# Turning the third group's alpha, q and k and the fourth group's alpha on four 64x64 tiles of TensorE

## The chip, the core and the metric

The kernel runs on one core of a Trainium2 chip. The core has five engines that run side by side and wait for each other through semaphores: TensorE (PE in the profile, with its weight loads as PEld), VectorE (DVE), ScalarE (ACT), GpSimd (POOL) and SyncE (SP, which here only issues DMAs). The metric is the time of one execution on the device, in microseconds; the kernel before took 270.44 us (median of 3 runs, 270.08 to 271.02).

## The reference

Two blocks follow each other. The first is a gated linear recurrence over 768 steps, for 4 batches and 8 heads of 48 numbers each. The second is a projection with a scalar decay, a gate and an output projection.

```python
for t in range(S):                       # attention block: B, H, S, D = 4, 8, 768, 48
    state = alpha[:, :, t, :, None] * state + np.einsum('bhd,bhe->bhde', k[:, :, t], v[:, :, t])
    y[:, :, t] = np.einsum('bhd,bhde->bhe', q[:, :, t], state)
x = y.transpose(0, 2, 1, 3).reshape(B, S, H * D)
proj = x @ w_in                          # 384 -> 2 * 512
val, gate = proj[..., :512], proj[..., 512:]
for t in range(S):
    h = np.exp(A_log)[0] * h + val[:, t, :]
    ys[:, t, :] = h
out = (gate * (1 / (1 + np.exp(-gate))) * ys) @ w_out
```

## The kernel before, in words

The work is cut into 12 groups of 256 steps: 4 batches with 3 groups each, counted m = 0 to 11. The recurrence of a group is done as matrix products: with running products of alpha, P (forward) and V (backward), q is scaled by P and k by V, then TensorE forms scores, masks them, multiplies by v, and carries a state from one 64-step part to the next. The second block of group n (`project`, four parts cc = 0 to 3, and `output`) runs on TensorE while the recurrence of group n + 1 is prepared.

The inputs arrive with steps along the free dimension: a raw tile has partition 4c + h (c one of 32 runs of 8 steps, h one of 4 heads) and, along the free dimension, the head group i (0 or 1), the step j in the run (0 to 7) and the 48 numbers d. The products need the numbers along partitions and the steps along the free dimension, so every alpha, q and k is *turned*. From the fifth group on (and for the k and q of the fourth) VectorE does it with 32x32 transposes (`turn`). For the first groups TensorE does it: it multiplies by an identity matrix (`ident`), the result lands in PSUM, and ScalarE copies it out in the order of the steps (`copy_turned`, line 714).

`turned` (line 697) turns half of a tensor, four of the eight steps j, into one PSUM bank. It has two ways. By matmul (line 707) each step j takes two products, one for each head group i: all 128 partitions of 64 columns of the raw tile are the weights, and the 128 columns of the identity move through, so a product fills 64 output partitions by 128 columns. By transpose (lines 702 and 703) a step takes two transposes. `turn_over` (line 764) calls it for the first four steps, copies the bank out, and then does the other four in a second bank. Its callers are `alphas` and `straighten`: alpha of group 1 (by transpose), k of group 0 (by transpose), and, what matters here, alpha (line 707), k and q (line 707) of group 2 and alpha of group 3 (by transpose, lines 702 and 703). The first alpha of all has a routine of its own, `first_alphas` (line 723), that works on 64x64 tiles.

Everything in this part of the kernel stands in an order written out by hand: each engine works through its own list, and no scheduler moves anything. Around the change, in the pass n = 0 of the main loop, TensorE's list is: `project(0, 0)`, alpha of group 2, `project(0, 1)`, scores of group 1, k of group 2, q of group 2, half of `project(0, 2)`, values across and states of group 1 (lines 834 and 866), the other half of `project(0, 2)`, alpha of group 3, the rest of group 1's values with the carried states (`third`: lines 847, 834, 847), and then, in the pass n = 1, scores of group 2 (line 798, 32 instructions into the banks s0 and s1 and 32 into two banks mm) and `project(0, 3)`. VectorE's list in the same stretch is: masks of group 1 (line 808), P of group 2 (line 635), V of group 2 (line 654), part of a weight's conversion (lines 549 and 551), the scan of `project(0, 2)` (line 995), four sums of states (line 894), and k and q of group 2 times V and P, in halves (lines 619 and 610); the scores of group 2 read these.

There are four PSUM banks mm0 to mm3 that are handed out in a written order (`taken`). k of group 2 takes banks 1 and 0, q of group 2 takes 2 and 3, `project(0, 2)` takes 1 and 0 and alpha of group 3 takes 2 and 3. SyncE issues the loads in their written order too; the raw tile of a tensor may be filled again once it has been turned.

Of the kernel before, what the change touches and what calls it, by code (L numbers as in the profile page):

```python
# [13 lines left out]
AF = mybir.ActivationFunctionType  # L14
# [332 lines left out]
def fast(  # L347
# [22 lines left out]
    nc = tc.nc  # L370
    B, H, S, D = q.shape
# [24 lines left out]
    NJ = GC // 32  # L396
    ROW = NJ * D
# [18 lines left out]
    def steps_of(name, m):  # L416
        return raws[name][:, ds(m % 2 * (2 * ROW + 16), 2 * ROW + 16)]
# [50 lines left out]
    ident = const.tile([C, C], FP32, name="ident")  # L468
# [127 lines left out]
    def by_runs(t):  # L596
        return t.rearrange("p h (c j) -> p h c j", j=NJ)
# [89 lines left out]
    def bank(tag=None):  # L687
        if tag:
            return ps_at.tile([C, 512], FP32, tag=tag, name=tag)
        return ps_mm.tile([C, 512], FP32, tag=f"mm{next(taken)}", name="mm")  # L690

    def bank_pair(tag=None):
        return [bank(tag and f"{tag}{i}") for i in range(2)]
# [3 lines left out]
    def turned(m, name, js, t, by_transpose=None):  # L697
        raw = steps_of(name, m)
        tp = t[:, 0:len(js) * C].rearrange("p (j x) -> p j x", j=len(js))
        if (m, name) in turned_by_transpose if by_transpose is None else by_transpose:  # L700
            for n, j in enumerate(js):
                nc.tensor.transpose(tp[:, n], raw[:, ds(ROW + j * D - 64, C)], ident)  # L702
                nc.tensor.transpose(tp[0:64, n], raw[:, ds(j * D, 64)], ident)  # L703
            return tp.rearrange("p j (c h) -> p h c j", h=4)
        for n, j in enumerate(js):
            for i in range(2):
                nc.tensor.matmul(tp[ds(64 * i, 64), n], raw[:, ds(i * ROW + j * D, 64)], ident,  # L707
                                 start=True, stop=True, skip_group_check=True)
        return tp.rearrange("p j (c h) -> p h c j", h=4)

    halves = [range(0, NJ // 2), range(NJ // 2, NJ)]

    def copy_turned(to, js, tp):
        nc.scalar.activation(by_runs(to)[:, :, :, js.start:js.stop], tp, AF.Copy)
# [47 lines left out]
        return to  # L762

    def turn_over(m, name, to):
        for js in halves:
            copy_turned(to, js, turned(m, name, js, bank()))

    def alphas(m):
        turn_over(m, "a", by_place(als[m % 2])[:, :, 1:GP])

    def straighten(m, name):
        to = plain(name)
        turn_over(m, name, to)
        return to
# [171 lines left out]
    for h in range(H):  # L946
        i, e, s = h // 4, h % 4 // 2, h % 2 ^ h // 4
# [183 lines left out]
    part = turned(1, "k", halves[0], bank())  # L1131
# [7 lines left out]
    part = turned(1, "k", halves[1], bank())  # L1139
# [9 lines left out]
    part = turned(1, "q", halves[0], bank())  # L1149
# [13 lines left out]
    part = turned(1, "q", halves[1], bank(), False)  # L1163
# [27 lines left out]
    for n in range(N):  # L1191
        m = n + 1
# [223 lines left out]
```

## Time and profile before

| what | value |
|---|---|
| median of 3 runs | 270.44 us (270.08 to 271.02) |
| the profiled execution | 269.92 us |
| span of the profile, first to last instruction | 268.2 us |
| TensorE busy | 263.3 us, 98% of the span |
| VectorE busy | 233.8 us, 87% |
| ScalarE busy | 111.6 us, 42% |
| GpSimd busy | 165.9 us, 62% |
| granted TensorE clock | 1.000 |

The profile is one execution. Its page gives the busy time of each engine, the chain of work that ended last (followed back from the last instruction, at each step to what released it), the costliest groups of instructions by source line, and the DMA issues. The trace behind it answers further questions: the chain in order of time, a timeline of one engine, or the instructions of one line. A row of a timeline reads: start in us, duration in us, engine, line, operation, output <- inputs, count, and in brackets the idle time before it and what ended that. A row that stands for several instructions (x32) runs from the first start to the last end. TensorE executes one fp32 product of the program as two rows of the trace; a transpose is one row. Matmuls are pipelined, so a row of the chain starts where the row before it ends, while the timeline shows the same group a little earlier, from its first start.

### The profile page before, as it was taken

What the parts mean: (1) busy time and instruction counts of PE and PEld (TensorE: products, weight loads), DVE (VectorE), ACT (ScalarE), POOL (GpSimd) and SP (SyncE); (2) the same over time, 40 slices, a digit from 0 to 9 for tenths busy, and PEclk for the clock granted to TensorE, in tenths of its full rate; (3) what the DMA queues carried; (4) which work ended last, traced back from release to release, by engine and by line L of the source; (5) the groups of instructions that cost most, each with busy time, mean ns of one, the idle gap of its engine ahead of it and who ended that gap; (6) DMA issues with size and microseconds to landing.
All of it is one profiled execution on the core that took longest, in us unless ns stands there. A gap on an engine that the chain in (4) does not pass through costs nothing.

```text
span 268.2 us, 9966 instructions
## 1 busy us (share of the span) xinstructions
PE 263.3 (98%) x4168; PEld 230.4 (86%) x4168; DVE 233.8 (87%) x316; ACT 111.6 (42%) x270; POOL 165.9 (62%) x185
## 2 busy tenths in 40 slices
PE   8999999999999999999999999999999999999995
PEld 6898889876688988988988988988988989988874
DVE  7979998996999999799999998999999998883440
ACT  4667766372342542532533533524524515214011
POOL 8222313084169997689985995996876986646000
PEclk9999999999999999999999999999999999999999
DMA  5947984998784569496487488569598501201101
GB/s 177 315 147 242 286 192 154 238 201 194 218 204 112 127 172 218 117 230 155 108 227 167 105 215 182 124 169 212 127 214 170 143 2 31 77 0 39 69 7 59
DMA packets 52304, 41.19 MB, mean 154 GB/s; under 512 B 27392, under 2 KB 50944, under 8 KB 52256
## 3 DMA queue, kind: packets, MB, share of 16 engines
q1 hardware_dynamic: 49328, 37.34, 56.2%
q0 software_dynamic: 1536, 2.20, 3.1%
q10 hardware_dynamic: 1392, 0.99, 1.3%
q8 instruction: 34, 0.56, 0.9%
q14 instruction: 14, 0.11, 0.1%
HBM read 32.54 MB, written 4.72 MB: 139 GB/s over the span
## 4 chain that ended last, share of the span: by engine, by line
PE 91%; DVE 2%; DMA 2%; issue 1%; ACT 1%; POOL 1%; SPq 0%; DVEq 0%; POOLq 0%
PE mm L988 47%; PE mm L1064 16%; PE y L834 4%; PE y L847 4%; PE mm L1022 4%; PE s L798 4%; PE mm L798 3%; PE s L866 3%; DMA raw_q<-in_q_dram 2%; PE mm L1377 2%; PE mm L707 1%; PE mm L702 1%; PE mm L703 1%; DVE P L635 1%; POOL w_in L556 1%
## 5 line engine op out<-in xcount | busy, mean ns | idle before, releaser
L988 PE MATMUL mm<-xT,w_in 128*128 128x256 f32 x576 | 129.5, 382 | 0.1
L988 PEld LDWEIGHTS mm<-xT,w_in 128*128 128x128 f32 x576 | 107.9, 190 | 15.9 <-issue 0.3
L1006 ACT ACTIVATE sg<-mm 128x256 f32<-128x256 f32 x48 | 18.4, 383 | 88.4 <-PE mm L988 85.3
L1008 POOL TENSOR_TENSOR f_last<-sg,hh 128x256 f32<-128x256 f32 x36 | 31.2, 874 | 24.2 <-ACT sg L1006 19.6
L886 POOL TENSOR_TENSOR sum<-sum,dS 128x192 f32<-128x192 f32 x30 | 37.5, 1251 | 3.0 <-ACT dS L874 1.4
L635 DVE TENSOR_TENSOR_SCAN P<-al,lower 128x1028 f32<-128x1028 f32 x12 | 30.3, 2521 | 0.3
L995 DVE TENSOR_TENSOR_SCAN hh<-a_dec,hh,mm 128x256 f32<-128x256 f32 x32 | 23.3, 728 | 7.8 <-PE mm L988 7.5
L654 DVE TENSOR_TENSOR_SCAN V<-al,ends 128x1028 f32<-128x1028 f32 x12 | 28.7, 2391 | 0.4
L963 POOL DMA_DIRECT2D xT<-yst x44 | 22.6, 519 | 4.9 <-ACT yst L960 3.7
L556 POOL TENSOR_TENSOR w_in<-w_in,wr 128x768 int32<-128x768 int32 x4 | 7.3, 1825 | 25.4 <-DVE wr L551 16.1
L1064 PE MATMUL mm<-wide,wr 128*128 128x192 f32 x108 | 20.8, 327 | 0.0
L818 POOL TENSOR_TENSOR AK<-AK,mask 128x512 f32<-128x512 f32 x9 | 15.6, 1729 | 7.7 <-ACT AK L814 7.6
L600 DVE STREAM_TRANSPOSE k<-raw_k 128x1024 f32<-128x1024 f32 x9 | 18.5, 2053 | 0.1
L600 DVE STREAM_TRANSPOSE q<-raw_q 128x1024 f32<-128x1024 f32 x9 | 18.3, 2035 | 0.0
L1064 PEld LDWEIGHTS mm<-wide,wr 128*128 128x128 f32 x108 | 18.0, 190 | 0.0
L874 ACT ACTIVATE dS<-s 128x384 f32<-128x384 f32 (+1 forms) x18 | 7.4, 461 | 22.3 <-PE s L866 22.3
L600 DVE STREAM_TRANSPOSE al<-raw_a 128x1024 f32<-128x1024 f32 x8 | 16.4, 2048 | 0.0
L619 DVE TENSOR_TENSOR Zk<-k,V 128x1024 f32<-128x1024 f32 (+1 forms) x14 | 16.1, 1148 | 0.1
L610 DVE TENSOR_TENSOR Zq<-q,P 128x1024 f32<-128x1024 f32 (+1 forms) x14 | 15.7, 1119 | 0.0
L1064 PE MATMUL mm<-w_out,f_last 128*128 128x192 f32 x72 | 15.6, 339 | 0.0
L847 PEld LDWEIGHTS y<-Zq,sum 48*64 48x64 f32 x656 | 11.6, 134 | 3.5 <-issue 3.2
L834 PEld LDWEIGHTS y<-AK,v 64*64 64x64 f32 x352 | 12.1, 134 | 2.9 <-issue 2.9
(188 smaller groups left out, 504.5 us busy)
## 6 DMA issues: line engine op xcount, KB each, us to landing
v<-in_v_dram SPq DMA_DIRECT2D x22, 192.0 KB, 3.8
out_dram<-o_sb SPq DMA_DIRECT2D x22, 192.0 KB, 2.5
raw_k<-in_k_dram SPq DMA_DIRECT2D x18, 184.0 KB, 4.7
raw_q<-in_q_dram SPq DMA_DIRECT2D x18, 184.0 KB, 4.5
raw_k<-in_k_dram SPq DMA_DIRECT2D x18, 176.0 KB, 5.0
raw_q<-in_q_dram SPq DMA_DIRECT2D x18, 176.0 KB, 4.8
wbits<-in_moe_w_in_dram SPq DMA_DIRECT2D x8, 384.0 KB, 4.9
raw_a<-in_alpha_dram SPq DMA_DIRECT2D x16, 184.0 KB, 3.6
```

Of the source, the lines that this page charges most:

```text
L600: nc.vector.transpose(out=by_runs(to).rearrange("p h c j -> p h j c"), in_=raws[name][:, 0:4 * ROW].rearrange("p (h j d) -> p h j d", h=4, ...
L635: nc.vector.tensor_tensor_scan(out=P, data0=al[:, 0:4 * GP], data1=lower.rearrange("p h t -> p (h t)"), initial=0.0, op0=ALU.mult, op1=ALU ...
L654: nc.vector.tensor_tensor_scan(out=V[:, ::-1], data0=al[:, 1:4 * GP + 1][:, ::-1], data1=ends.rearrange("p h t -> p (h t)")[:, ::-1], init ...
L798: nc.tensor.matmul(scs[m][c][i][ds(L * h, L), ds(p * (L + D), L + D)], Zk[rows, c, p, ds(h * L, L)], Zq[rows, u, p], start=True, stop=True ...
L834: nc.tensor.matmul(ys[m][i][ds(64 * s, 64), e, ds(c * C + h * L, L)], v_sb[rows, c, 4 * i + p, :], As[i][rows, c, p, :], start=across and ...
L847: nc.tensor.matmul(ys[m][i][ds(64 * s, 64), e, ds(u * L, L)], Ss[j][rows, p, :], Zqs[m % 2][rows, u, p, D:], start=False, stop=True, skip_ ...
L886: nc.gpsimd.tensor_add(Ss[j][:, :, 0:D], Ss[j - 1][:, :, 0:D], part)
L963: engines[n % len(engines)].dma_start(out=xT[to, a], in_=st[rows, i, e])
L988: nc.tensor.matmul((pv, pg)[vg], w_ins[cc][:, kk, vg, :], xT[:, kk, :], start=(kk == 0), stop=(kk == NK - 1))
L995: nc.vector.tensor_tensor_scan(out=hh, data0=a_dec[:, cc:cc + 1].to_broadcast([C, GC]), data1=pv, initial=prev_h[cc][:, GC - 1:GC] if n % ...
L1008: f = lambda: engine.tensor_mul(fs[n][cc], sg, hh)
L1064: nc.tensor.matmul(o, a[:, k], b[k] if type(b) is list else b[:, k], start=start and k == 0, stop=k == KC - 1, skip_group_check=True)
```

## The change

`turn_over` keeps the old way for groups 0 and 1. For groups 2 and 3 it takes two banks at once, one for each half of the 128 partitions (r = 0: the first 128 steps of the group, r = 1: the other 128). For each step j it makes four products, one for each pair of head group i and row half r: 64 partitions of 64 raw columns are the weights, and the 64x64 block of the identity on the same partitions moves through. A product fills 64 output partitions by 64 columns of the bank of its row half. When all 32 products of the tensor are listed, ScalarE copies the two banks out, each as 128 consecutive steps. Alpha of group 3 is no longer turned by transposes. The number of copies and the order in which banks are handed out are the same, and no other list changes.

```diff
     def turn_over(m, name, to):
-        for js in halves:
-            copy_turned(to, js, turned(m, name, js, bank()))
+        if m < 2:
+            for js in halves:
+                copy_turned(to, js, turned(m, name, js, bank()))
+            return
+        raw = steps_of(name, m)
+        parts = [t.rearrange("p (j x) -> p j x", x=64) for t in bank_pair()]
+        for j in range(NJ):
+            for i, r in ((0, 0), (1, 1), (1, 0), (0, 1)):
+                rows = ds(64 * r, 64)
+                nc.tensor.matmul(parts[r][ds(64 * i, 64), j], raw[rows, ds(i * ROW + j * D, 64)],
+                                 ident[rows, rows], start=True, stop=True, skip_group_check=True)
+        for r, part in enumerate(parts):
+            nc.scalar.activation(by_runs(to)[:, :, ds(16 * r, 16)], part.rearrange("p j (c h) -> p h c j", h=4), AF.Copy)
```

## The prediction

> **What bounds the kernel now.** I read the page first, for the shares and for the engine that the chain of waits follows.
>
> ```profile
> span 268.2 us, 9966 instructions
> PE 263.3 (98%) x4168; PEld 230.4 (86%) x4168; DVE 233.8 (87%) x316; ACT 111.6 (42%) x270; POOL 165.9 (62%) x185
> PE 91%; DVE 2%; DMA 2%; issue 1%; ACT 1%; POOL 1%; SPq 0%; DVEq 0%; POOLq 0%
> ```
>
> TensorE is busy for 98% of the span and makes up 91% of the chain, so time taken from it ought to come off the end. VectorE, at 87%, is close behind. Averages don't say which of the two is ahead in the stretch that changes, so I then read the chain in order of time, from 25 us on.
>
> ```profile
> 25.37 1.83 POOL w_in L556
> 27.25 2.86 PE mm L988 x12
> 31.80 3.64 PE mm L707 x64
> 35.44 1.49 PE mm L988 x6
> 36.94 0.62 PE y L834 x32
> ...
> 39.77 0.11 PE mm L702
> ...
> 41.41 0.11 PE mm L703
> 41.52 0.39 PE y L847 x16
> 41.91 0.47 PE y L834 x32
> 42.38 0.70 PE y L847 x48
> 43.08 0.77 PE s L798 x32
> 43.85 0.77 PE mm L798 x32
> 44.61 1.49 PE mm L988 x6
> ```
>
> From 27.25 us on every piece is TensorE's and each begins where the last one ends. The turning of k and q (L707, x64) is a piece of 3.64 us; alpha of group 3 (L702 and L703) lasts from 39.77 to 41.52, 1.75 us. Alpha of group 2 is no piece of the chain: before 27.25 stands GpSimd's sum for a weight (L556).
>
> The third view is the stretch from the end of this turning to the end of what can be delayed by it, and asks whether TensorE ever stands after 44.6 us.
>
> ```profile
> 44.60:264.00 219.40, 219.40 (x3232) 192.12 (x3231) 193.94 (x244) 82.63 (x207) 151.12 (x164) 1.00 0.60 141
> ```
>
> The first two numbers are the length of the stretch and TensorE's busy time in it: both 219.40. Whatever TensorE has gained when it starts on `project(0, 3)` at 44.6 us, the end gains too, as long as the other engines follow. So the question is only how much earlier it gets there. The fourth view, VectorE's timeline, answers that.
>
> ```profile
> 32.52 2.58 DVE L635 TENSOR_TENSOR_SCAN P<-al,lower 128x1028 f32<-128x1028 f32 x1
> ...
> 35.56 2.30 DVE L654 TENSOR_TENSOR_SCAN V<-al,ends 128x1028 f32<-128x1028 f32 x1
> ...
> 39.31 1.61 DVE L894 TENSOR_TENSOR sum<-s,sum 128x192 f32<-128x192 f32 x4
> 40.83 0.68 DVE L619 TENSOR_TENSOR Zk<-k,V 128x512 f32<-128x512 f32 x1
> 41.43 0.68 DVE L610 TENSOR_TENSOR Zq<-q,P 128x512 f32<-128x512 f32 x1
> 42.03 0.68 DVE L619 TENSOR_TENSOR Zk<-k,V 128x512 f32<-128x512 f32 x1
> 42.64 0.68 DVE L610 TENSOR_TENSOR Zq<-q,P 128x512 f32<-128x512 f32 x1
> 43.90 0.42 DVE L808 TENSOR_TENSOR A<-s,mask 128x256 f32<-128x256 f32 x1 [0.58 <-PE s L798]
> ```
>
> Up to 43.32 us (42.64 + 0.68) no row carries a bracket: VectorE goes from one instruction to the next without waiting for anybody, and nothing it reads in this stretch comes late. Its next row waits 0.58 us for the scores. TensorE and VectorE are therefore nearly level at 43 us, and TensorE's lead over what VectorE supplies is the measure of what it can gain:
>
> ```profile
> 42.90 0.95 PE L798 MATMUL s<-Zq,Zk 48*64 48x112 f32 x32
> 43.67 0.95 PE L798 MATMUL mm<-Zq,Zk 48*64 48x112 f32 x32
> ```
>
> The second half of the scores of group 2 starts at 43.67 and reads the Zq that is ready at 43.32. That is 0.35 us of room, no more.
>
> **The change part by part.** *One tensor on 64x64 tiles.* 32 products, two rows each: 64 rows in place of 32 (alpha, k and q of group 2), and in place of 16 for alpha of group 3, whose transposes are one row each. TensorE's count grows by 3 x 32 + 48 = 144 rows, to 4312. The nearest rows are the values of L834, which also rotate through all four tiles with 64 columns: 32 in 0.47 us (41.91), 14.7 ns a row, and 0.62 us (36.94) where they follow 128-row work, so 0.15 us for the step into this mode. The other end is the routine that does the same job for the first alpha, at the very start:
>
> ```profile
> 5.13 0.68 PE L723 MATMUL y<-ident,raw_a 64*64 64x64 f32 x26
> L723 PEld LDWEIGHTS s<-ident,raw_a x32: 175/223/228, 3.9 to 5.0; 64*64 64x64 f32 x32
> L723 PE MATMUL y<-ident,raw_a x32: 218/218/311, 4.8 to 5.6; 64*64 64x64 f32 x32
> ```
>
> There 26 rows last 0.68 us; less the 0.218 us of the last one, 25 intervals are 18.5 ns each. All 64 rows of that routine, from 3.9 to 5.81 us, take 30 ns each, the earlier ones with weight loads at 223 ns. I take 14.7 ns, because the new order also changes both the row half and the column half, as L834 does; 30 ns is the upper end.
>
> *k and q:* 128 x 14.7 ns = 1.88 us for 3.64, so 1.76 us less. No step into the mode is added, since L798 before them already runs on parts of the array. *Alpha of group 3:* 64 x 14.7 + 150 = 1.09 us for 1.75, so 0.66 us less. *Alpha of group 2:* gains nothing, as what follows it waits for GpSimd until 25.37 + 1.83 = 27.20, and ScalarE is not free for its copies earlier either:
>
> ```profile
> 26.97 0.36 ACT L1006 ACTIVATE sg<-mm 128x256 f32<-128x256 f32 x1
> 27.23 1.36 ACT L714 ACTIVATE al<-mm 128x512 f32<-128x512 f32 x2
> ...
> 32.64 0.33 ACT L810 ACTIVATE dS<-mm 128x192 f32<-128x192 f32 x1
> 32.87 0.60 ACT L714 ACTIVATE k<-mm 128x512 f32<-128x512 f32 x1
> ...
> 35.49 0.60 ACT L714 ACTIVATE q<-mm 128x512 f32<-128x512 f32 x1 [0.28 <-PE mm L707]
> ```
>
> *Both banks at once.* q needs bank 3 with its second product. Bank 3 is freed by the copy dS, at 32.97; k's tiles would be done at 31.80 + 0.94 = 32.74, so q waits about 0.25 us with the handover (between 0 and 0.3). `project(0, 2)` then starts near 34.0 on banks 1 and 0, and the first copy of k, 0.60 us from about 33.0, has freed bank 1 by 33.6; no wait.
>
> *The copies.* Same count, same size, 0.60 us each. The first can no longer begin halfway, so a tensor's last copy ends 1.2 us after its products instead of 0.9. Its cover: Zk reads k from 40.83 on, where the copies now end at 35.5 to 36.1 and would end near 35.4. If a copy took twice as long, q's would end near 38, still covered.
>
> *SyncE.* The reload of raw k waits for k's turning, but also stands behind loads of v:
>
> ```profile
> 30.46 3.72 SPq L441 DMA_DIRECT2D v<-in_v_dram  x2
> 34.28 1.90 SPq L411 DMA_DIRECT2D raw_k<-in_k_dram  x3
> v<-in_v_dram SPq DMA_DIRECT2D x2, 192.0 KB, 5.6
> ```
>
> So it doesn't move. v of group 1 is the pair of loads before these two, issued before 30.46 and 5.6 us on the way; it lands at 35 to 36 us; the values of group 1 would start near 35.5. A wait up to 0.6 us can appear there, in front of slack.
>
> *The sum.* TensorE reaches the carried states (now 41.52) earlier by 1.76 - 0.25 + 0.66 = 2.17 us, at 39.35. There it waits for the first of VectorE's four sums, at 39.31 + 0.40 = 39.71. It then needs 0.39 + 0.47 + 0.70 = 1.56 us and is at the scores at 41.3, where it waits for the first halves of Zk and Zq until 41.43 + 0.68 = 42.11. Their 32 rows of 0.77 us end at 42.94, and the second half waits until 43.32. With 0.05 us for a handover (GpSimd's end at 27.20 to TensorE's start at 27.25) it starts at 43.37 in place of 43.67: **0.30 us are gained, of 2.17 us saved**; the rest becomes waits of about 0.4, 0.8 and 0.4 us before 43.4 us. Any row price below 25 ns gives the same sum, because VectorE sets it. The profiled execution took 269.92 us, 1.7 more than its span, and would take 269.62. The median of the runs shown is 0.52 above it; from there I forecast **270.14 us**.
>
> **The rivals.** *VectorE does not hold it back (faster).* If its list ended earlier, TensorE's whole saving could come through: 270.44 - 2.17 = 268.3 us. In its favour: P took 2.58 us at 32.52 where V took 2.30, so rows there are not all at their shortest, and 0.28 us of that would make 269.9. Against it: nothing in the change touches VectorE's list or what it reads, and for the rest its rows would have to shrink by 1.9 us.
>
> *The waits slow the clock (slower).* TensorE has no idle time in this stretch now. It would stand for about 1.6 us out of the 4 us up to 43.4. What a slow clock costs, the start shows:
>
> ```profile
> L779 PE MATMUL y<-const-float32-0.0 x6: 634/634/782, 1.0 to 3.3; 128*128 128x256 f32 x6
> L988 PE MATMUL mm<-xT,w_in 128*128 128x256 f32 x576 | 129.5, 382 | 0.1
> ```
>
> The same shape took 634 ns there and 382 later, and the slow phase lasted from 1.0 to about 5.1 us. Once more such a phase of 4.1 us costs 4.1 x (1 - 382/634) = 1.63 us: 271.8 us. It decides only if the waits together are enough to bring it on; each alone is under 1 us. [...]
>
> *The tiles are slow (slower).* At 30 ns, 192 rows on the chain take 5.76 us; with the 0.15 and 0.25 us that is 6.16 for 5.39, so TensorE is 0.77 us late, and nothing covers that: 271.2 us. It turns from gain to loss at 26 ns. Against it: 14.7 ns in 32 rows at 41.91 and 18.5 in the same job.
>
> *The gain is lost again.* Some engine has less than 0.30 us of room after 44.6: 270.44 us, no change.
>
> **How the numbers follow.** Forecast 0.60, VectorE no bound 0.14, slow clock 0.11, slow tiles 0.08, lost again 0.07. About 0.3% (0.8 us) is what a measurement of this kernel can tell from no change. Faster by more needs a time below 269.6: most of the 0.14, and a twentieth from the spread of the runs, 0.18. Slower by more, above 271.25: the 0.11 and a part of the slow tiles, 0.15. Within it: 0.67. The range runs from 269.3, a part of the first rival with it, to 271.2, the slow tiles; outside it lie the slow clock and the deep end of the first rival.
>
> **What would show it.** Right: tiles of k and q as one stretch of about 2.1 us from 31.7; `project(0, 2)` starting near 34.0; TensorE idle before L847, and twice before scores of group 2; Zq ending at 43.3 as now; no new wait after 44 us. Wrong: a granted clock under 1.0 or longer rows after 40 us; VectorE's Zq ending elsewhere than at 43.3; rows of the new line more than 25 ns apart; `project(0, 2)` waiting for a copy; any bracket on TensorE after 45 us.

## The result and the profile after

The changed kernel takes 272.21 us (median of 6 runs, 271.26 to 274.39) where the kernel before, timed beside it, takes 270.31 us (6 runs, 270.08 to 271.02): ratio 1.0078, 95% interval 1.0055 to 1.0102. It is slower, clear of the noise. A ratio leaves out executions more than 1.5% above the fastest of their kernel; in this document these are two of the changed kernel's second run, 278.43 and 278.76 us. The profiled execution is the longest of the six, 274.39 us. From its page: the span, TensorE's row, the granted clock in 40 slices, and the DMA queue called q8 (packets, MB, share of the span).

```profile
span 272.7 us, 10261 instructions
PE 263.6 (97%) x4312; PEld 230.3 (84%) x4312; DVE 232.6 (85%) x316; ACT 111.2 (41%) x270; POOL 165.8 (61%) x185
PEclk9997999999999999999999999999999999999999
...
q8 instruction: 35, 0.57, 1.0%
```

The count is the forecast's 4312, and TensorE's busy time is what it was (263.3 before), so the time did not go into the work of the tiles: the span grew by 4.5 us and TensorE's share of it fell. The chain of waits in order of time (start, duration, what) shows where:

```profile
30.20 1.09 PE mm L774 x64
31.29 2.79 PE mm L999 x12
...
35.77 1.22 PE mm L774 x66
37.00 0.91 PE mm L774 x42
37.91 0.35 issue
38.26 0.57 PE mm L774 x17
38.82 1.49 PE mm L999 x6
...
43.15 1.09 PE mm L774 x64
44.24 0.23 PE y L858 x16
44.48 0.47 PE y L845 x32
44.94 0.23 PE y L858 x15
45.18 1.42 issue
46.60 0.73 PE y L858 x33
47.33 0.77 PE s L809 x32
```

(Lines behind the change are 11 higher than before: scores L809, values L845, carried states L858, `project` L999; the tiles are L774.) In the kernel before, this part of the chain is TensorE without a break. Now there are two pieces called "issue": 0.35 us in the middle of q's tiles and 1.42 us in the middle of the 48 products of L858, between two products of one kind with the same inputs at hand. "issue" is time in which an engine waits for nothing that the profile shows. The list of TensorE's waits (total, times, longest) has two more of the kind, at 20.6 and 17.0 us, ahead of the first changed instruction:

```profile
PE y L937 <- issue: 1.9, 1, 1.9
PE y L858 <- issue: 1.4, 1, 1.4
...
PE y L929 <- issue: 0.5, 1, 0.5
PE mm L774 <- issue: 0.4, 1, 0.4
```

What these four places share is found by counting. Three stretches, each from the end of one stall to the end of the next (TensorE's matmuls and weight loads are the counts behind the first two times; a window also counts a neighbour that is still running at its edge):

```profile
17.43:22.53 5.10, 3.16 (x128) 2.81 (x128) 3.14 (x4) 1.76 (x5) 1.81 (x1) 1.00 0.53 163
22.53:38.26 15.73, 15.37 (x381) 13.46 (x380) 11.61 (x18) 10.53 (x22) 3.63 (x2) 0.89 0.90 258
38.26:46.60 8.34, 6.92 (x256) 5.79 (x255) 8.03 (x15) 4.80 (x9) 1.83 (x1) 1.00 0.53 148
```

Counted in the order of their starts, with the instructions on semaphores that the trace also lists for TensorE (2, 8 and 3 of them), the instructions behind the stalls are 256, 768 and 512 apart. The stalls lie at multiples of 256 TensorE instructions. And q8 moves 0.57 MB in 35 packets, 16 KB each, one for every 256 of TensorE's 4312 + 4312 instructions and 101 on semaphores (8725 / 256 = 34.1). So, by these counts, q8 brings TensorE's own instructions.

How a block comes to be late is seen at the larger of the two stalls behind the change. TensorE passes a boundary at 42.77 us. The next packet, by its order the block behind the next boundary, is on q8 from 43.98 to 45.35 us, and the first of that block's instructions runs at 46.60. A window around the packet shows it, 5.9% of 16 engines in 1.45 us, which is 1.37 us of one:

```profile
q8 instruction: 1, 0.02, 5.9%
```

So 3.8 us lie between passing one boundary and being able to pass the next: 1.2 until the packet starts, 1.4 on the way, 1.25 until it runs. TensorE used up its 256 instructions in 2.19 us:

```profile
42.77:44.96 2.19, 2.19 (x129) 1.88 (x127) 1.99 (x6) 1.07 (x3) 1.71 (x1) 1.00 0.13 36
```

In the kernel before, the same boundaries lie at 42.60 and 47.82 us (the counts include neighbours that are still running at the edges), and 5.22 us are enough:

```profile
42.60:47.82 5.22, 5.22 (x142) 4.48 (x136) 4.52 (x9) 3.10 (x9) 2.07 (x4) 1.00 0.47 153
```

The change put 288 more instructions into this part of the kernel and made the stretch around a boundary dense.

### The profile page after: what moved, and what is told of

Its sections match the earlier page's. It is cut to its first block, busy times and chain, and to the rows that moved or that the text cites. A ratio compares the mean times of both kernels' runs of the same rounds, so it can differ in the third digit from the quotient of the medians.

```text
span 272.7 us, 10261 instructions
## 1 busy us (share of the span) xinstructions
PE 263.6 (97%) x4312; PEld 230.3 (84%) x4312; DVE 232.6 (85%) x316; ACT 111.2 (41%) x270; POOL 165.8 (61%) x185
## 4 chain that ended last, share of the span: by engine, by line
PE 93%; DVE 3%; issue 2%; DMA 1%; ACT 0%; ACTq 0%; DVEq 0%
PE mm L999 47%; PE mm L1075 16%; PE y L845 4%; PE y L858 4%; PE mm L1033 4%; PE mm L809 3%; PE s L809 3%; PE s L877 3%; PE mm L1388 2%; PE mm L774 2%; DMA raw_a<-in_alpha_dram 1%; PE y L937 1%; PE y L929 1%; DVE V L654 1%; DVE P L635 1%
## 5 line engine op out<-in xcount | busy, mean ns | idle before, releaser
L999 PE MATMUL mm<-xT,w_in 128*128 128x256 f32 x576 | 129.5, 382 | 0.0
L999 PEld LDWEIGHTS mm<-xT,w_in 128*128 128x128 f32 x576 | 107.9, 190 | 15.5 <-issue 0.2
L1075 PE MATMUL mm<-wide,wr 128*128 128x192 f32 x108 | 20.8, 327 | 0.0
L1075 PEld LDWEIGHTS mm<-wide,wr 128*128 128x128 f32 x108 | 18.0, 190 | 0.0
L858 PEld LDWEIGHTS y<-Zq,sum 48*64 48x64 f32 x656 | 11.8, 134 | 4.9 <-issue 4.5
L858 PE MATMUL y<-Zq,sum 48*64 48x64 f32 x656 | 14.3, 221 | 1.4 <-issue 1.4
L1075 PE MATMUL mm<-w_out,f_last 128*128 128x192 f32 x72 | 15.6, 339 | 0.0
L619 DVE TENSOR_TENSOR Zk<-k,V 128x1024 f32<-128x1024 f32 (+1 forms) x14 | 15.1, 1080 | 0.1
## 6 DMA issues: line engine op xcount, KB each, us to landing
v<-in_v_dram SPq DMA_DIRECT2D x22, 192.0 KB, 3.8
out_dram<-o_sb SPq DMA_DIRECT2D x22, 192.0 KB, 2.6
```

Of the source, the lines that this page charges most:

```text
L858: nc.tensor.matmul(ys[m][i][ds(64 * s, 64), e, ds(u * L, L)], Ss[j][rows, p, :], Zqs[m % 2][rows, u, p, D:], start=False, stop=True, skip_ ...
L999: nc.tensor.matmul((pv, pg)[vg], w_ins[cc][:, kk, vg, :], xT[:, kk, :], start=(kk == 0), stop=(kk == NK - 1))
L1075: nc.tensor.matmul(o, a[:, k], b[k] if type(b) is list else b[:, k], start=start and k == 0, stop=k == KC - 1, skip_group_check=True)
```

## The experiments

Three theories to begin with. A: TensorE's instructions arrive in blocks of 256, and a stretch that runs through a block in less than about 3.7 us (an estimate near the 3.8 us above) leaves it standing. B: idle time of whatever origin slows TensorE's clock, and that is the cost (the forecast's rival). C: the two early stalls belong to the one execution. Later A was sharpened to A2: what counts is where the boundaries fall against the dense stretches of the whole kernel, those far behind the change too.

**The two kernels once more.** No edit.

> The changed kernel, once more. Theory A (TensorE's instructions are fetched in pages of 256, and a page that TensorE runs through in under about 3.5 us leaves it standing until the next page is there): stalls of some 0.4 and 1.4 us end at the page boundaries near 37.7 and 45 us in every profile, about 1 us lost, 271.0 to 271.8 us without anything else. Theory B (TensorE's idling slows the clock): every run that is over 271 us shows a mean clock under 1. Theory C (the stalls near 16.7 and 20.4 us and the slow clock after them, all before the first changed instruction, belong to that one execution and not to the change): they are absent in this profile or shorter, and then the time is under 272 us.

> The kernel before, once more, as a measure of how often an unchanged program shows the early stalls. Theory C: its profile may show an early stall at instruction 448 or 704 of TensorE too, since its second page ends its fetch only 1.5 us before the first instruction of the next page runs; its times then reach 271 us and more now and then. Theory A: no stall after 30 us, 270.1 to 270.6 us.

The changed kernel: 273.57 us (median of all eleven executions), ratio 1.0073 [1.0045, 1.0102], more than theory A expected (at most 271.8). The kernel before as a run of its own: 270.56 us, 1.0002 [0.9970, 1.0035]. B as the whole cost fails here: two executions of the changed kernel took 272.53 and 273.64 us at a mean clock of 1.000. The profiled execution of the changed kernel took 278.76 us; it is used for its stalls and the clock behind them, not for its time. From its list of waits:

```profile
PE y L858 <- issue: 3.5, 1, 3.5
...
PE mm L774 <- issue: 0.8, 1, 0.8
PE y L845 <- issue: 0.8, 1, 0.8
```

The stalls at L774 and L858 are there again at the same instructions, the early ones at L929 and L937 are not. C holds for this pair of profiles, but the one at L937 came back, with 0.6 us, in a later run (the load of w_out later) whose instructions up to there are those of the changed kernel: it comes and goes from execution to execution. (The boundary that held L937 exists in the kernel before too, where TensorE takes 2.93 us for that block and the packet was early enough.) The kernel before has no wait on "issue" in its list at all.

**Parts of the change alone.** k and q of group 2, alpha of group 3, alpha of group 2 on tiles, everything else as before:

```diff
-        if m < 2:
+        if m < 2 or name == "a":          # k and q alone
+        if (m, name) != (3, "a"):         # the fourth alpha alone
+        if (m, name) != (2, "a"):         # the third group's alpha alone
```

> Only k and q of group 2 in the new way, both alphas in the old one. Theory A: the 256 instructions of k and q are a whole page in 2.1 us and the page with the scores of group 2 is short too; TensorE stands 0 to 0.7 us near 35.4 and 0.4 to 1.1 us near 43, so -0.3 to +0.8 us against the kernel before, most likely +0.3. If instructions cost nothing (the forecast's reading): -0.3 us.

> Only alpha of group 3 in the new way. Theory A: the page that begins near 41.3 holds the carried states, values and scores of group 2 and is run through in 2.9 us; TensorE stands 0.3 to 1.0 us near 44.2, so 0 to +0.7 us against the kernel before. If instructions cost nothing: the room of 0.30 us is used, -0.3 us.

> Only the third group's alpha is turned on 64x64 tiles; k, q and the fourth alpha stay as before. It is the tensor for which the forecast saw nothing on the path. Theory A: 64 more TensorE instructions before 32 us move every later boundary of 256 by 64 places; the stretch around 30 to 34 us ran with slack before, so no stall over 0.5 us there; the boundary that fell at instruction 1984 now falls 64 instructions earlier in the work, where the k and q products are still half columns, so the stall is at most 0.5 us and the time is 270.2 to 271.2 us. Theory B alone: the same, 270.4 us. If every added tile costs alike wherever it stands: a quarter of the loss of the whole change, 270.9 to 271.2 us.

k and q alone: 274.27 us, 1.0112 [1.0058, 1.0166]. The fourth alpha alone: 276.24 us, 1.0199 [1.0132, 1.0266]. The third group's alpha alone: 272.82 us, 1.0108 [1.0064, 1.0151]. The first two are far above what theory A expected (0.8 us more than before at most). The fourth alpha alone costs more than the whole change, clear of the noise, and the other two at least about as much, so the costs don't add up, and a cost per tile or per row that is the same wherever it stands is excluded. For k and q, the chain shows VectorE's Zq ready in time and then a stall inside the scores:

```profile
42.59 0.61 DVE Zq L610
43.24 0.61 PE mm L809 x15
43.85 1.35 issue
45.20 1.09 PE mm L809 x17
```

A second one, of 0.69 us, ends at 131.1 us.

For the fourth alpha, stalls at 42.15, 46.90, 133.09 and 173.19 us (their ends) are 256, 2560 and 1280 instructions apart. The last two stretches, with 25 and 14 semaphore instructions (and a neighbour at the edge of the second window):

```profile
46.90:133.09 86.19, 84.87 (x1267) 71.25 (x1268) 77.59 (x92) 32.14 (x74) 56.35 (x58) 0.98 0.73 172
133.09:173.19 40.10, 39.12 (x634) 35.06 (x634) 37.52 (x40) 15.68 (x40) 29.44 (x34) 1.00 0.72 165
```

The last two lie 90 and 130 us behind the last changed instruction, in work that no edit touched. The third group's alpha, which the forecast had cost at nothing, has no stall near the change at all and two late ones, at 167 and 208 us, in the products of `output` (L1075):

```profile
PE mm L1075 <- issue: 1.9, 2, 1.6
```

Its time lies above what each of the three readings expected (271.2 us at most), though the stretch near the change has no stall, as A had it; that gave A2. The 64 instructions that it adds move every later boundary by 64 places, and boundaries that lay harmlessly in the kernel before come to lie ahead of dense stretches.

**The load of w_out later.** The changed kernel; SyncE asks for the first 768 KB of w_out behind the four transfers of xT that `third` ends with, at 49.73 us in place of 43.68, so that this transfer leaves the time of the late packet.

```diff
-            load_w_out(0, nc.sync)
             ...
+            load_w_out(0, nc.sync)        # behind third(m)
```

> The changed kernel with one edit: SyncE asks for the 768 KB of w_out of the next pass behind the loads of the third group instead of ahead of them, so that this transfer no longer lies around 40 to 44 us. Theory A (TensorE's instructions come in packets of 256 on the queue called q8, and stretches of many short instructions overtake them; other transfers make the packets later still): the packet that belongs to TensorE's instruction 1984, which started 1.3 us (changed kernel), 4.56 us (its second run), 2.4 us (k and q alone) and 3.0 us (fourth alpha alone) after TensorE had crossed the boundary before it, now starts about 1.3 us after it; TensorE's stall there shrinks from 1.4 to 3.5 us to 0.5 to 1.2 us, no half clock follows it, and the time is 270.5 to 271.8 us. Rival A' (the packet is late by TensorE's pace alone, the transfer beside it is innocent): the stall stays at 1.3 us or more, and the time at 271.8 to 273.6 us. Theory B alone (the forecast's rival: idle time of any origin slows the clock) gives no reason for any change: 272 to 273.6 us.

274.87 us, 1.0144 [1.0105, 1.0182]. The packet started 1.30 us after the boundary, as A expected, but it had done so in the first profile of the changed kernel too, without the edit, and the stall stayed, with 1.6 us. For the stall, rival A' held; the time is above what any of the theories expected. That the transfer makes the packet late is therefore not shown by this run. (The 4.56 and 3.0 us in the expectation were counted from before a stall at the boundary; from the boundary itself they are 3.55 and 2.3.) The expectation of a stall of 0.5 us had not been worked through: 3.9 us from boundary to boundary less 2.1 us of work is 1.8. New in its list of waits, and not in the changed kernel's, are two for VectorE and GpSimd (0.8 and 0.6 us); they stand between 66 and 91 us:

```profile
PE mm L774 <- issue: 1.6, 1, 1.6
PE y L858 <- issue: 1.6, 1, 1.6
...
PE mm L999 <- DVE hh L1006: 0.8, 1, 0.8
PE y L937 <- issue: 0.6, 1, 0.6
PE y L858 <- POOL sum L897: 0.6, 1, 0.6
```

**More products without tiles.** The kernel before, each half-column product of k and q of group 2 issued as two of 64 moving columns: the same bank layout and the same columns through TensorE, but 128 more instructions.

```diff
-                nc.tensor.matmul(tp[ds(64 * i, 64), n], raw[:, ds(i * ROW + j * D, 64)], ident, ...)
+                for cols in (ds(0, 64), ds(64, 64)) if m == 2 and name in "kq" else (ds(0, C),):
+                    nc.tensor.matmul(tp[ds(64 * i, 64), n, cols], raw[...], ident[:, cols], ...)
```

> The kernel before, in which k and q of the third group are still turned on half columns, but each of their 64 products is issued as two of 64 moving columns: 128 products for 64 in the same two tensors, the same columns through TensorE as before, no 64x64 tile and no row halves in two banks. Theory A (the count of TensorE's instructions in a stretch is what costs): as with k and q alone on tiles, TensorE stands 1 to 3.5 us between 43 and 47 us at the boundary that ends at its instruction 1984, and the time is 271.2 to 274.3 us against 270.5 before. Rival (something of the 64x64 tiles themselves or of the two banks costs the time): no stall over 0.25 us, and the time within 0.4 us of the kernel before (270.1 to 270.9 us), since the products' time on TensorE is that of before.

273.01 us, 1.0104 [1.0036, 1.0173], as k and q on tiles. The two stalls, inside scores at 46.1 and 130.1 us (their ends), lie at the same instruction numbers as the two of k and q on tiles:

```profile
PE mm L799 <- issue: 1.6, 2, 1.2
```

No 64x64 tile and no row halves in two banks are needed for the loss; more instructions are enough. (The split products of k and q also take 3.93 us on TensorE where they took 3.64 before, so 0.29 us of it is their own; the stalls are 1.6.)

**The same halves with fewer instructions.** The changed kernel's row halves, banks and copies, but each row half turned by transposes, one row of the trace each: 4184 matmuls, 16 more than before.

```diff
-            for i, r in ((0, 0), (1, 1), (1, 0), (0, 1)):
-                nc.tensor.matmul(parts[r][ds(64 * i, 64), j], raw[rows, ds(i * ROW + j * D, 64)], ident[rows, rows], ...)
+            for r in range(2):
+                nc.tensor.transpose(parts[r][:, j], raw[rows, ds(ROW + j * D - 64, C)], ident[rows, rows])
+            for r in range(2):
+                nc.tensor.transpose(parts[r][0:64, j], raw[rows, ds(j * D, 64)], ident[rows, rows])
```

> The changed kernel with the same tensors, the same row halves in two banks and the same copies by ScalarE, but with both column blocks of a row half turned where possible by one instruction (a 64-row transpose to 128 partitions, and one to 64 for the rest), so that each tensor takes 64 TensorE instructions' worth of two sizes instead of 64 products with their own weight loads: the row that the trace gives for the tensor's products will tell how many instructions of the page it is. Theory A: with at most as many TensorE instructions as the kernel before in these stretches, no stall over 0.5 us stands at the boundary of instruction 1984, and the time is 269.8 to 271.2 us; by the forecast's bound (VectorE lets the scores of the third group start at most 0.30 us earlier) it cannot be under 269.9 us by more than the measurement tells. Rival (row halves, two banks or ScalarE's copies by halves cost the time): stalls of 1 us or more between 43 and 47 us and 272 us or more.

270.09 us, 0.9994 [0.9967, 1.0022]: the loss is gone but for one stall of 0.4 us at L860, and no gain can be measured. Its chain shows the forecast's bound at work:

```profile
42.82 0.61 DVE Zq L610
43.44 0.04 issue
43.48 1.00 PE mm L811 x32
44.48 2.79 PE mm L1001 x12
```

The second half of the scores starts as soon as VectorE's Zq is ready, at 43.48, where the forecast had 43.37; `project(0, 3)` starts at 44.48 in place of 44.61.

**Small products ahead of all work.** To move the boundaries without touching any later work, small products of zeros (64x16) were put into the warm-up, in place of one, none and two of its three wide products.

```diff
+        for _ in range(short):
+            nc.tensor.matmul(t[0:16, 0:16], zeros[64, 16], zeros[64, 16], ...)
-    keep_warm(3, 256)
+    keep_warm(2, 256, 48)     # kernel before
+    keep_warm(3, 256, 8)      # kernel before
+    keep_warm(1, 256, 104)    # third group's alpha alone
+    keep_warm(1, 256, 76)     # k and q alone
```

> The kernel before with nothing changed but its warm-up: the last of three 128x256 products of zeros is replaced by 48 small ones (64x16 tiles), 96 more TensorE instructions ahead of all work and none later. Theory A2 (what counts is where the boundaries of 256 TensorE instructions fall against the short-instruction stretches of the whole kernel; the kernel before has no stall because its boundaries happen to fall well): every boundary now comes 96 instructions earlier in the work. Laid over the starts of the kernel before, with a page released 3.7 us after the boundary ahead of it is reached by an engine that looks some 32 instructions ahead, three boundaries come too early, near 45, 129 and 169 us, by about 1 us each: stalls at instruction numbers that are 193 beyond a multiple of 256, 2.0 to 4.3 us together, and 272.3 to 275 us against 270.5. Rival (the stalls belong to the tiles and the added products of the change): no stall beyond the first 10 us, 270.2 to 271.2 us.

> The same with 8 small products behind the three wide ones, 16 more TensorE instructions ahead of all work. Theory A2: laid over the starts of the kernel before, boundaries that come 16 instructions earlier all fall well: no stall over 0.3 us and 270.2 to 270.9 us, so that it is not the added instructions as such that cost. If any added instruction at the start costs by itself (a later start, a later warm-up), a sixth of what 48 products cost.

> The third group's alpha alone on 64x64 tiles (the experiment that stood 1.82 us at 167 us and 0.59 us at 208 us), with 104 small products in the place of two of the three warm-up products: 208 more TensorE instructions ahead of all work, 272 with the alpha's 64. Theory A2: the boundaries behind the alpha then fall 16 instructions from where the kernel before has them, and the two stalls go; one of about 0.4 us is left near 19 to 20 us. The time falls from 272.8 us to 270.3 to 271.3 us, with more instructions than before. Rival (each added instruction costs, or the alpha's tiles do): 272.8 us or more.

> k and q of the third group alone on 64x64 tiles (the experiment with 274.3 us), with 76 small products in the place of two warm-up products, 152 more TensorE instructions ahead of all work. Theory A2: laid over that experiment's starts, boundaries 152 instructions earlier leave 0.2 to 0.5 us of stalls, all of it near 20 us, and none at 43 to 47 us or 130 us: 270.2 to 271.2 us. It would also be the place where a gain of the tiles shows, at most the 0.30 us that the forecast found VectorE to allow. Rival (tiles in the stretch of 37 to 43 us cost wherever the boundaries lie): 272 us or more.

276.94 us, 1.0214 [1.0188, 1.0241]; 271.49 us, 1.0029 [1.0015, 1.0043]; 283.12 us, 1.0458 [1.0415, 1.0501]; 276.63 us, 1.0236 [1.0177, 1.0294]. The expectations all missed, for two reasons that are mine. One fp32 product is two matmuls and two weight loads, so 48 of them are 192 instructions and not 96; and they are slow at the start and push the first turning back (5.66 us here, 3.9 and 4.32 in the two profiles of the kernel before):

```profile
2.99 2.74 PE L783 MATMUL y<-const-float32-0.0 64*16 64x16 f32 x96
5.66 1.19 PE L723 MATMUL s<-ident,raw_a 64*64 64x64 f32 x30
```

In the first of the four, work is 2.3 us later from 25 to 85 us; the two with 104 and 76 products start turning at 7.80 and 6.30 us, so their times hold several us that no boundary explains. With 8 products, two stalls came where none was expected, 0.8 us at 23.4 and 0.3 us at 56.8 us (their ends). The second shows that a long block is not safe by itself: TensorE worked 7.4 us through that block and stood all the same, as the packet started 5.1 us after the boundary while the DMA engines were full (share 0.92 until the packet):

```profile
49.05:54.13 5.08, 5.08 (x90) 4.55 (x83) 4.70 (x12) 1.19 (x3) 0.00 (x0) 1.00 0.92 236
...
PE y L838 <- issue: 0.3, 1, 0.3
```

What remains is one fact: with 48 products the unchanged kernel got a stall of 2.57 us between two products of `output`, at a multiple of 256, some 185 us behind the only edit:

```profile
190.11 0.59 PE L1068 MATMUL mm<-w_out,f_last 128*128 128x192 f32 x2
193.28 0.48 PE L1068 MATMUL mm<-w_out,f_last 128*128 128x192 f32 x2 [2.57 <-POOL AK L822]
```

The bracket names GpSimd's AK, which these products don't read; their packet came in at 192.0 us, and they start 1.26 us later, like the others.

**Fewer instructions at the start.** The clean form of the test: the first group's alpha, which has 64x64 tiles in both kernels, is turned by the transposes of above. That takes 64 instructions away from ahead of everything and adds none.

```diff
-        for j in range(NJ): ... turn_quarter(j, i, r)
+        for j in range(NJ):
+            for r in range(2):
+                nc.tensor.transpose(tps[j // 4][r][:, j % 4], raw[rows, ds(ROW + j * D - 64, C)], ident[rows, rows])
+            for r in range(2):
+                nc.tensor.transpose(tps[j // 4][r][0:64, j % 4], raw[rows, ds(j * D, 64)], ident[rows, rows])
```

> The kernel before with one edit at its start, outside the change: the first group's alpha, which is turned on 64x64 tiles, is turned by transposes of its row halves (to 128 partitions and to 64), which takes 64 TensorE instructions fewer (matmuls and weight loads as the trace counts them: 128 rows become 64). Theory A2: all later boundaries of 256 now fall 64 instructions later in the work. Laid over the starts of the kernel before (a page released 3.6 to 3.8 us after the engine, looking 24 to 40 instructions ahead, reaches the boundary ahead of it), stalls come at instructions 705 (near 20 us, 0.3 to 0.6 us), 6337 (near 187 us, 0.7 to 1.0 us or more if transfers delay the packet) and 7617 (near 227 us, 0.3 to 1.4 us), where the kernel before has none: 271.3 to 273.7 us against 270.5, with fewer instructions. Rival (the tiles and instructions that the change adds are the cause, boundaries are not): 270.5 us or, with 64 instructions fewer, up to 1 us less, no stall over 0.25 us behind 30 us.

> The third group's alpha alone on 64x64 tiles (272.8 us, stalls of 1.82 us at 167 us and 0.59 us at 208 us), with the first group's alpha turned by 64 TensorE instructions fewer as in the run beside it. Theory A2: behind the third group's alpha all boundaries fall within an instruction of where the kernel before has them; both stalls go, one of 0.25 to 0.6 us may be left near 20 us: 270.2 to 271.2 us. Two edits that each cost about 2 us alone then cost nothing together. Rival (costs of the edits add up): 273 us or more.

> The fourth alpha alone on 64x64 tiles (276.2 us, stalls of 0.5, 2.1, 1.5 and 1.2 us at 42, 45, 132 and 172 us), with the first group's alpha turned by 64 TensorE instructions fewer. Theory A2: of the four stalls at most 0.2 us at 42 us and 0.25 to 0.6 us near 20 us is left, since behind the fourth alpha the boundaries fall where the kernel before has them: 270.2 to 271.4 us, 5 us less than without the edit at the start. Rival (the tiles of the fourth alpha cost where they stand): 274 us or more.

The kernel before with this edit: 275.92 us, 1.0168 [1.0097, 1.0240], slower with fewer instructions. The third group's alpha with it: 271.34 us, 1.0019 [0.9996, 1.0043], where it cost 1.0108 without. The fourth alpha with it: 271.18 us, 1.0016 [0.9994, 1.0038], where it cost 1.0199. Two edits that cost 1.7% and 2.0% alone cost nothing that can be measured together. That is what A2 says and what no cost of the tiles can say. In the first of the three, the stall is at the boundary that A2 had named (instruction 6337, near 187 us), one product from where the kernel with 48 small products stands in the same work (6337 + 64 = 6401 against 6593 - 188 = 6405, counted as in the kernel before):

```profile
187.78 0.95 PE L792 MATMUL mm<-Zq,Zk 48*64 48x112 f32 x32
191.82 1.44 PE L1058 MATMUL mm<-w_out,f_last 128*128 128x192 f32 x4 [3.09 <-POOL AK L812]
```

Its size was taken too small: 3.1 us for 0.7 to 1.0, because the packet started 3.1 us after the boundary in place of some 1.3, while the DMA engines were full (share 0.90 to 1.09 from 185 to 189.5 us). With it the time, 275.92 us, is above the range expected (273.7 at most). The one named near 20 us came (0.2 us), the one near 227 us did not. Behind this one TensorE ran 6.18 us at a granted clock of 0.52:

```profile
191.82:198.00 6.18, 6.18 (x21) 6.18 (x21) 1.86 (x1) 2.52 (x8) 0.59 (x1) 0.52 0.34 68
```

The start itself also comes later: in the profiles, work from 50 us on is 1.9 us later in the first of the three (until the stall), 1.3 us in the second and not at all in the third. So part of the first one's loss is not the boundaries'. The fourth alpha's run has no "issue" of weight left in its list; all its waits over 0.25 us are:

```profile
PE y L784 <- PEq L1405: 1.0, 1, 1.0
PE mm L744 <- DMA raw_q<-in_q_dram: 0.7, 2, 0.5
PE s L724 <- DMA raw_a<-in_alpha_dram: 0.5, 1, 0.5
```

**All together.** Instructions more than before are twice the difference in matmuls to 4168; what counts for the far boundaries is their remainder by 256.

| kernel | more | remainder | ratio to before |
|---|---|---|---|
| third group's alpha, start shortened | 0 | 0 | 1.0019 |
| row transposes | 32 | 32 | 0.9994 |
| before, 8 small products | 32 | 32 | 1.0029 |
| fourth alpha, start shortened | 32 | 32 | 1.0016 |
| the change | 288 | 32 | 1.0078 |
| third group's alpha | 64 | 64 | 1.0108 |
| fourth alpha | 96 | 96 | 1.0199 |
| k and q | 128 | 128 | 1.0112 |
| k and q in halves, no tiles | 128 | 128 | 1.0104 |
| k and q, 76 small products | 424 | 168 | 1.0236 |
| before, 48 small products | 188 | 188 | 1.0214 |
| before, start shortened | -64 | 192 | 1.0168 |
| third group's alpha, 104 small products | 472 | 216 | 1.0458 |

Every kernel with a remainder from 0 to 32 is within 0.3% of the one before, but for the change itself, and every other one is over 1% slower (the three with many small products, and the kernel before with its start shortened, partly by a late start). The change leaves the far boundaries nearly where they were and loses only in the stretch that it made dense; its parts alone lose in unchanged work as well.

## Why the prediction was wrong

*What bounds the kernel.* Right as far as it went: TensorE's unbroken chain and VectorE's list. "Whatever TensorE has gained ... the end gains too, as long as the other engines follow" is where it broke. Another supplier was left out, that of TensorE's instructions, though the page had it as a queue, with 34 packets and 0.9% of the DMA engines' time.

*One tensor on 64x64 tiles.* This is the step that failed. It counted 144 rows more and priced them as rows; their other price, put at nothing, is 288 instructions, more than one block of 256, in and just ahead of the densest part of the kernel. Measured: stalls of 0.35 us in q's tiles and 1.42 us in L858, 1.77 us together, in the profiled execution (0.8 and 3.5 in the second, 1.6 and 1.6 with the load of w_out moved). The tiles' own price lay within the forecast's bounds of 14.7 to 30 ns a row: alpha of group 3 took 1.09 us, exactly as forecast; k and q took 1.22 + 0.91 + 0.57 = 2.70 us for the forecast's 1.88 with 0.25 of waiting, 21 ns a row, below the 26 ns at which the sum turns. So TensorE saved 0.94 + 0.66 = 1.60 us and lost 1.77. Most of the profiled execution's 4.5 us came ahead of that: 4.0 us were there when k's tiles began (35.77 us in place of 31.80), from the stalls at 17.0 and 20.6 us and the slow clock behind them (granted 0.50 from 23.51 to 26.92 us). How the 1.9 us between the two medians divide among the stalls is not shown, since the other timed executions have no trace; that the added instructions bring them is shown by the row transposes, which take most of these instructions away and the loss with them, and by the split products, which add instructions without any tile and lose about as much as k and q on tiles.

*Alpha of group 2 gains nothing.* True for the tensor and false for the sum: at nothing it was priced by what waits for it, and its 64 instructions move every later boundary. Alone it cost 1.0108.

*Both banks at once, the copies, SyncE.* No wait of the changed kernel is put down to any of them; the few on copies of k are 0.2 us long and stand in the kernel before too.

*The sum.* VectorE's bound was right, and the runs without stalls at 45 us show it: scores at 43.48 and 43.51 us (the fourth alpha with the start shortened), forecast 43.37. So 0.30 us was all there was to gain; 0.13 came through in the row transposes. In the changed kernel the three waits of 0.4, 0.8 and 0.4 us never appeared, as TensorE was late and not early.

*The rivals.* The slow clock gave 271.8 us, the nearest number, by another mechanism than what happened: it wanted the waits for VectorE to bring it on. Its 1.63 us took the rows of 634 ns at the start for rows at a slow clock; that is an estimate of mine, since the granted clock reads 1.00 there (1.00 to 5.10 us). Four of the six timed runs had a mean clock of 0.998 or more and were 271.3 to 272.5 us, so most of the loss is there without it. In the profiled execution the granted clock was 0.50 from 23.51 to 26.92 us, behind a stall of 1.93 us that ended at 22.53. Slow tiles, at 21 ns, did not decide. Of the signs listed as against the forecast, two came: a bracket on TensorE after 45 us, and Zq ending at 46.99 us and not at 43.3, because everything was some 4 us late by then. In the second profile the granted clock also fell to half behind 47 us (0.70 from 47 to 48 us, 0.50 from 48 to 49), after the stall of 3.5 us.

## What to carry to other kernels

An engine that is 98% busy with short instructions has a second supply to watch: count its instructions, matmuls and weight loads apart, and ask of each run of 256 whether it lasts longer than the next block needs to come (here 3.8 us from boundary to boundary with the DMA engines nearly idle, and 8.1 us at L845 in the second profile of the changed kernel). A shorter run is a risk and not a certainty: runs of 2.1 and 2.3 us passed without a stall in the kernel before (from 183.66 and 144.42 us), where the packet had started 3.0 and 2.3 us ahead of the boundary. Replacing one instruction by two that are each half as long can lose where a stall follows (1.0104 for the split products). And in a kernel tuned to the last per cent an edit of a few dozen instructions can cost 1 to 2% far behind the place where it stands (1.0108 for 64, 1.0199 for 96), so look for "issue" at multiples of 256 before blaming the edit, and move the boundaries with another edit before dropping it.

## What the runs showed of the hardware that was not expected

- At the stall that ends at 46.60 us in the profiled execution of the changed kernel, the DMA engines were nearly idle from the boundary to the packet (share 0.07 from 42.77 to 43.98 us). There 3.8 us lie between the time TensorE passes a boundary and the time it can pass the next: the packet starts 1.2 us after the boundary, takes 1.4 us, and the first instruction runs 1.25 us after its end. At the stalls that end at 38.26 and 22.53 us, with shares of 0.80 and 0.50, it was 0.8, 1.1 and 1.3 us, 3.2 in all, and 2.0, 1.7 and 1.4 us, 5.1 in all; at L845 in the second profile it was 8.1 us in all (about 55.35 to 63.45 us). Behind the first 20 us of the profiles of the kernel before and of the changed kernel, stall or no stall, the packets that had a share under 0.1 from the boundary to their start began 0.4 to 1.3 us after it, and those that began more than 2.0 us after it (2.1 to 3.9 us) had a share of 0.86 or more, but most of those that began 1.1 to 1.9 us after it had 0.75 to 1.16 too; that the transfers cause the lateness is read from these figures and not shown. Some packets start ahead of the boundary, at most 35 instructions ahead in the kernel before and 38 in the changed kernel; where one started 3.0 us ahead (180.66 for 183.66 us in the kernel before), a block of 2.13 us needed no stall.
- The granted clock fell to half for 3.41 us (23.51 to 26.92 us) behind the stall of 1.93 us in the profiled execution of the changed kernel. The stalls of 2.2 us (the fourth alpha), 2.6 us (48 small products), 3.1 us (the kernel before with its start shortened), 3.2 us (104 small products) and 3.5 us (the second profile of the changed kernel) stand in profiles with a mean clock of 0.994, 0.994, 0.988, 0.993 and 0.986, worth 3.3, 3.3, 6.6, 3.9 and 7.8 us at half by an estimate ((1 - clock) x 2 x span), wherever in the profile they stand. After a shorter stall, of 1.35 us, it fell too (k and q alone: 0.59 from 45 to 46 us, 0.50 to 48 us), but not after the one of 1.42 us in the profiled execution (1.00 from 46.60 to 270 us), and the profiles with stalls of 1.2 us (the split products) and 1.6 us (the third group's alpha) have a mean clock of 1.000.
- A releaser named by the profile can be a coincidence: two stalls of 2.57 and 3.09 us (48 small products, start shortened) bore the name of GpSimd's AK, and one of 2.2 us (the fourth alpha) that of ScalarE's dS, while all three stood at a boundary of 256; the first of them ended 1.26 us after its packet.
